# Expert weights in memory of their own, and the first expert unit chosen and turned while attention still runs

## The chip, the cores and the metric

The kernel runs on one core of a Trainium2 chip. The core has five engines that each take their instructions in order and wait for one another by semaphores: TensorE (PE, matrix products; PEld is its weight load), VectorE (DVE), ScalarE (ACT), GpSimd (POOL) and SyncE (SP, which here only starts DMAs). DMAs are started from SP, ACT and POOL. The metric is the time of one execution in device microseconds (us); lower is better. The kernel before took 1386.26 us, the median of three runs (1385.36, 1386.26, 1387.59).

## The reference: what is computed

Three stages follow one another, all in float32. The first is a decayed attention of 8 batches of 576 tokens with 8 heads of 64, the second a top-1 mixture of 8 experts (512 to 1024 to 512), the third a dense layer with a gate (512 to 2048 to 512).

```python
scores = scale * np.matmul(q, k.transpose(0, 1, 3, 2))
Dmat = np.where(rel >= 0, gamma[:, None, None] ** rel[None, :, :], 0.0)
x = np.matmul(scores * Dmat, v)                # then to (4608 tokens, 512)
logits = x @ w_gate + modality_bias[modality_id]
e_idx = np.argmax(logits, axis=1)              # gate_w: its softmax weight
for e in range(E):
    mask = e_idx == e
    out[mask] = gate_w[mask, None] * (np.maximum(x[mask] @ w1[e], 0.0) @ w2[e])
h = out @ w_in
result = (h - np.tanh(h)) @ w_out
```

Which tokens an expert gets is known only once attention and routing have run.

## The kernel before

**Attention.** 36 tiles of 128 tokens run in the loop of line 575, four tiles to a group (`RG`), groups 0 to 8. Tile `t` issues the scores of tile `t + 1` (`scores`), its own products (`attend`), the copy of its result to `xt` (`evac_x`, L433, on DVE), the scaling of a later tile's values on POOL, and the load of tile `t + 6` on SP (`load_tile`, six buffers from a pool). Routing of group `g - 1` is spread over the tiles of group `g`: `route_a` (logits, L464, copied by ACT at L467), `route_b` (turned, maximum, one-hot; L473 to L489), `route_c` (ranks by prefix sums, L498 to L516; L512 keeps the running counts `cum`). Then, a tile at a time, `scatter` writes token numbers into the slot table in DRAM by an indirect DMA on POOL (L520), and `store_x` turns a tile on PE (L531), scales it on ACT (L536, `save_x`) and writes it to `x_d`. The rule `due` doubles the scatters and stores up for group 6, so that tiles 24 to 27 are in DRAM early.

**The first unit.** An expert unit is up to 390 rows of one expert (`UE`); there are 12 of them, and a loop for what is left over. Since the first unit needs a full 390 rows before all are routed, `choose` (L436) takes the expert with the most rows among the first 28 tiles. Before, it stands at the end of tile 31. At tile 33 SP reads the choice into a register and loads the row numbers (`load_ids`, L199), and POOL fetches the rows in four pieces (`gather_rows`, L203; the last has 6 rows). After the last tile come the four turns of these rows on PE (`early`, L161, split by ACT at L162 and DVE at L163 into a high and a low float32r part), `route_a` of group 8, and the turn of tile 28.

**Expert units.** `blocks` (L700) runs steps `i` of (unit, f), f = 0 to 7. A step is 12 matmuls of 128x390 (L714: high by high, low by high, high by low, for four parts of the contraction), then `post` (relu on ACT at L824, low part on DVE at L825, weights of later steps split at L792 and L793), then `prep` (what else is due), and 12 matmuls of the second product of step `i - 2` (L943 to L945). The weights of a unit lie in `raw`, 16 pieces of 128x512, eight loads of 512 KB; `raw` and the split parts `wh` and `wl` came from pools opened after attention had closed its own. The first three loads of unit 0 were issued by SP after the last tile (L783), the other five by ACT in `post` of steps 0 and 1. The rest of the routing is hung into `prep` of unit 0: `rest_a` after step 0 (three scatters, `route_b` of group 8, two rows of stores), `rest_b` after step 1 (`route_c`, stores, four scatters), `rest_c` after step 2 (the counts by L642, `table`, L662 to L685 on DVE, which makes the list of units `utab`, and four stores), and then `swap`, which closes attention's right-hand pools. Unit 1's row numbers are loaded after step 2 (L199), its rows fetched after step 3 (L203) and turned after steps 6 and 7 (`tr_x`, L161). Later units fetch their rows in 13 pieces and turn them on DVE.

**PSUM.** Eight banks: in attention three for scores, two for the results, one for the state and two (`ps_m`) for routing and stores. In the units four are `hp` (a step's first product, and the tiles that `late_x` turns, in rotation) and four `acc`.

**The dense stage** (L982 to L1058) has 9 blocks of 512 tokens with 16 steps each; its weights `wout` (16 tiles) are loaded as it begins.

## Time and profile before

| | us |
|---|---|
| median of three runs | 1386.26 |
| lowest, highest | 1385.36, 1387.59 |
| the profiled execution | 1377.49 |
| its span, first to last instruction | 1375.8 |
| PE busy in the span | 1351.2 (98%) |
| DVE, ACT, POOL busy | 1041.5, 695.2, 330.5 |
| TensorE clock granted, mean | 0.997 of full |

The profile is of one execution, some 9 us below the median of the timed runs. Times in it count from the span's start. A row of the timeline gives the start, the time that it takes, the engine (with a q for what its queue issues), the line, the operation and its operands; `x8` is a merged row of eight; `[0.56 <-DVE rk L506]` is idle time of the engine just before it and what ended that. A float32 product of attention or a transpose by float32 counts several records. Ends on PE are modelled: two matmuls of 128x390 that follow each other start 0.18 us apart though each row says 0.34.

Attention takes the span up to 154.25 us, the units from 160.88 us to about 600 us, the dense stage the rest.

### The profile page before, as it was taken

The page shows a single profiled execution, that of the slowest core. Times are in us where ns is not written, and L with a number is a line of the kernel's source. Part 1 is how long each engine was busy: PE and PEld are TensorE (multiplying, and loading weights), DVE is VectorE, ACT ScalarE, POOL GpSimd, SP SyncE. Part 2 cuts the span into 40 slices and gives each one's busy share as a digit, 9 for nine tenths or more (in the row PEclk, how much of TensorE's full clock was granted, in tenths as well). Part 3 has the DMA queues.
Part 4 walks back from the last instruction along what each step waited for, and adds up shares of the span by engine and source line. Part 5 has one row for each costly group of instructions (what it writes and reads, how often), then busy time and mean ns, then how long its engine had stood idle before and what let it go on. Part 6 is the DMA issues. An engine that isn't in the chain of part 4 may idle for free.

```text
span 1375.8 us, 22319 instructions
## 1 busy us (share of the span) xinstructions
PE 1351.2 (98%) x8267; PEld 1186.1 (86%) x8267; DVE 1041.5 (76%) x1684; ACT 695.2 (51%) x1232; POOL 330.5 (24%) x381
## 2 busy tenths in 40 slices
PE   8999799999999999999999999999999999999998
PEld 7888699899999999988888888888888888888886
DVE  5766477798889888568778777786776877778775
ACT  3333344444444444456656556555555655555643
POOL 4555242443444444101101111011100111011101
PEclk9999999999999999999999999999999999999999
DMA  9998457444843446270100001000000000000000
GB/s 370 411 330 295 134 173 214 153 139 139 237 136 95 96 124 201 55 254 31 54 8 31 31 1 43 19 31 31 1 31 31 31 31 0 32 31 0 31 1 31
DMA packets 79726, 140.77 MB, mean 102 GB/s; under 512 B 36112, under 2 KB 42832, under 8 KB 79612
## 3 DMA queue, kind: packets, MB, share of 16 engines
q1 hardware_dynamic: 58780, 83.99, 18.7%
q10 hardware_dynamic: 12096, 35.45, 8.0%
q0 software_dynamic: 8736, 19.86, 4.3%
q8 instruction: 66, 1.08, 0.3%
q14 instruction: 48, 0.39, 0.1%
HBM read 133.29 MB, written 39.55 MB: 126 GB/s over the span
## 4 chain that ended last, share of the span: by engine, by line
PE 51%; issue 5%; POOL 0%; POOLq 0%; ACT 0%
PE hp L714 26%; PE acc L1021 8%; PE acc L1022 8%; PE acc L1023 8%; POOL out_dram L1047 0%; POOLq L1073 0%; ACT o L1044 0%; POOL nopt L1046 0%; POOLq L1037 0%; POOLq L1047 0%
## 5 line engine op out<-in xcount | busy, mean ns | idle before, releaser
L994 ACT ACTIVATE eh<-hp 128x512 f32<-128x512 f32 x144 | 86.1, 598 | 293.2 <-PE hp L714 274.9
L714 PE MATMUL hp<-xh,winh 128*128 128x512 f32 x576 | 224.1, 389 | 0.1
L1021 PE MATMUL acc<-wout,hi 128*128 128x512 f32 x576 | 224.2, 389 | 0.0
L1023 PE MATMUL acc<-wout,lo 128*128 128x512 f32 x576 | 224.2, 389 | 0.0
L1022 PE MATMUL acc<-wout,hi 128*128 128x512 f32 x576 | 224.1, 389 | 0.0
L714 PE MATMUL hp<-xl,winh 128*128 128x512 f32 x576 | 224.1, 389 | 0.0
L714 PE MATMUL hp<-xh,winl 128*128 128x512 f32 x576 | 224.1, 389 | 0.0
L996 DVE TENSOR_TENSOR el<-eh,hp 128x512 f32<-128x512 f32 x144 | 99.0, 688 | 156.5 <-ACT eh L995 156.5
L194 POOL DMA_INDIRECT xg<-x_d,idt x130 | 149.9, 1153 | 196.8 <-DVE lo L825 70.1
L742 POOL TENSOR_TENSOR xl<-yr,xh 128x512 fp32r<-128x512 f32 x36 | 49.2, 1366 | 429.2 <-ACT xh L741 429.2
L824 ACT ACTIVATE hi<-hp 128x390 fp32r<-128x390 f32 x96 | 47.7, 496 | 185.5 <-PE hp L714 132.5
L1005 DVE SCALAR_TENSOR_TENSOR el<-eh,el 128x512 f32<-128x512 f32 x144 | 128.6, 893 | 15.4 <-DVE el L1004 0.5
L714 PE MATMUL hp<-xh,wl 128*128 128x390 f32 x384 | 130.9, 341 | 3.4 <-DVE wl L793 3.4
L714 PE MATMUL hp<-xh,wh 128*128 128x390 f32 x384 | 132.0, 344 | 2.2 <-ACT wh L792 2.2
L714 PE MATMUL hp<-xl,wh 128*128 128x390 f32 x384 | 131.3, 342 | 0.2 <-issue 0.2
L943 PE MATMUL acc<-hi,wh 128*128 128x390 f32 x384 | 131.3, 342 | 0.0
L944 PE MATMUL acc<-lo,wh 128*128 128x390 f32 x384 | 130.5, 340 | 0.0
L945 PE MATMUL acc<-hi,wl 128*128 128x390 f32 x384 | 129.8, 338 | 0.2 <-issue 0.2
L714 PEld LDWEIGHTS hp<-xh,winh 128*128 128x128 f32 x576 | 108.2, 188 | 22.8 <-issue 0.4
L714 PEld LDWEIGHTS hp<-xh,winl 128*128 128x128 f32 x576 | 108.2, 188 | 22.6
L1022 PEld LDWEIGHTS acc<-wout,hi 128*128 128x128 f32 x576 | 108.3, 188 | 22.5
L1023 PEld LDWEIGHTS acc<-wout,lo 128*128 128x128 f32 x576 | 108.1, 188 | 22.7 <-DVE lo L1000 0.4
(169 smaller groups left out, 2611.9 us busy)
## 6 DMA issues: line engine op xcount, KB each, us to landing
raw<-in_w_dram SPq DMA_DIRECT2D x91, 512.0 KB
qk<-in_qk_dram SPq DMA_DIRECT2D x36, 512.0 KB
vk<-in_vk_dram SPq DMA_DIRECT2D x36, 512.0 KB
y_d<-yo SPq DMA_DIRECT2D x12, 780.0 KB
yr<-y_d SPq DMA_DIRECT2D x9, 1024.0 KB
raw<-in_wo_dram ACTq DMA_DIRECT2D x16, 512.0 KB
wo_d<-cv_em ACTq DMA_DIRECT2D x16, 512.0 KB
raw<-in_wi_dram ACTq DMA_DIRECT2D x16, 512.0 KB
```

The source lines that it names most:

```text
L194: nc.gpsimd.indirect_dma_start(out=dst, out_offset=None, in_=x_d[0:NT, :].rearrange("t (q c) -> (t q) c", q=NQ), in_offset=bass.IndirectOf ...
L714: nc.tensor.matmul(out=hp, lhsT=lhs, rhs=rhs, start=j == 0, stop=j == 3 * KD - 1)
L742: nc.gpsimd.tensor_tensor(out=yl[:, k], in0=yr[:, k], in1=yh[:, k].bitcast(F32), op=ALU.subtract)
L943: nc.tensor.matmul(out=o, lhsT=wh[:, cs], rhs=hi, start=first, stop=False)
L944: nc.tensor.matmul(out=o, lhsT=wh[:, cs], rhs=lo, start=False, stop=False)
L945: nc.tensor.matmul(out=o, lhsT=wl[:, cs], rhs=hi, start=False, stop=last)
L994: nc.scalar.activation(out=u, in_=hp, func=ACTF.Square)
L996: nc.vector.tensor_tensor(out=v, in0=u, in1=hp, op=ALU.mult)
L1005: nc.vector.scalar_tensor_tensor(out=v, in0=s, scalar=SQ_C, in1=v, op0=ALU.add, op1=ALU.mult)
L1021: nc.tensor.matmul(out=acc[s], lhsT=hi, rhs=wh, start=first, stop=False)
L1022: nc.tensor.matmul(out=acc[s], lhsT=hi, rhs=wl, start=False, stop=False)
L1023: nc.tensor.matmul(out=acc[s], lhsT=lo, rhs=wh, start=False, stop=last)
```

## The change

The weights of the first unit and the split buffers get memory that is taken at the start (`home`), so that their loads need not wait for attention's pools. The choice of the first unit moves from tile 31 to tile 30, the loading of row numbers and rows from tile 33 to tile 31, the eight weight loads into tiles 32 to 35 (all on ACT's queue), and three of the four turns into tiles 34 and 35. So that the choice can come earlier, routing of group 6 is pulled into tiles 28 and 29 (three scatters at tile 28, four at tile 29) and its stores into tiles 28 to 30. Routing of group 8 moves a step later: `route_a` after step 0, `route_b` after step 1, `route_c` inside `post` of step 2, the counts and `table` ahead of step 3; `swap` and unit 1's row numbers come after step 3. The first unit's rows now lie in a buffer of `xt` instead of two of the `vk` buffers. In the dense stage `raw` also serves as scratch, as input from block 1 on and as output buffer, six of the 16 `wout` tiles take the place of the split buffers, and the pool of `hi` and `lo` has three buffers instead of four.

```diff
+        home = pool("home", 1)
+        raw = home.tile([128, 2 * F1, DM], F32, name="raw")
+        w_b = [[home.tile([128, 2, DM], F32R, name=f"{n}{i}") for n in ("wh", "wl")] for i in range(3)]
...
+            def load_first(f):
+                nc.scalar.dma_start(out=raw[:, 2 * f:2 * f + 2].rearrange("p h c -> p (h c)"),
+                                    in_=A["w12"][bass.ds(first_act, 1), f, 0].rearrange("o p c -> (o p) c"))
...
+                soon = g == EARLY
                 if t + 1 < NTILE:
                     scores(t + 1)
+                if soon and r == 0:
+                    ls_box[g - 1] = route_a(g - 1)
+                if t == NTILE - 2:
+                    turn_rows(0, 0, x0[0], ps_sc.tile([128, KD, TL], F32, name="sc"))
+                if t == NTILE - 1:
+                    for s in range(1, SE - 1):
+                        turn_rows(0, s, x0[s], ps_m.tile([128, KD, TL], F32, name="m"))
                 attend(t)
...
+                if soon and r == 0:
+                    route_b(g - 1, ls_box.pop(g - 1))
+                    for w in range(t - RG - 3, t - RG):
+                        scatter(w)
+                elif soon and r == 1:
+                    route_c(g - 1)
+                    for w in range((g - 1) * RG, g * RG):
+                        scatter(w)
...
+                    for w in ([w], [w, w + 1], [w + 1, w + 2, w + 3], [])[r] if soon else [w]:
+                        store_x(w)
-                if t == (EARLY + 1) * RG - 1:
+                if t == EARLY * RG + 2:
                     choose()
-                if t == (EARLY + 1) * RG + 1:
+                if t == EARLY * RG + 3:
                     base = nc.sync.value_load(pick[0:1, 0:1], min_val=0, max_val=(E - 1) * CAP)
-                    first = nc.sync.value_load(pick[0:1, 1:2], min_val=0, max_val=E - 1)
                     first_act = nc.scalar.value_load(pick[0:1, 1:2], min_val=0, max_val=E - 1)
...
+                if t >= EARLY * RG + 4:
+                    for f in ((0,), (1, 2), (3, 4), (5, 6, 7))[t - EARLY * RG - 4]:
+                        load_first(f)
+                if t >= NTILE - 2:
+                    split_w((t - NTILE + 2, 0))
...
-            early(0)
-            early(1)
-            ls_last = route_a(g)
-            for s in range(2, SE):
-                early(s)
-            t_ahead = late.pop(0)
-            tp_ahead = turn_x(t_ahead, False)
             c1.close()
...
+                    else:
+                        for _ in range(2):
+                            h_p.tile([128, UB], F32, name="hp")
+                        t = late.pop(0)
+                        tp = turn_x(t, True)
+                        turn_rows(0, SE - 1, x0[SE - 1], h_p.tile([128, UB], F32, name="hp").rearrange("p (k t) -> p k t", k=KD))
+                        ahead.extend((t, tp))
+                        split_w((2, 0))
+                    blocks(names, F1, 2, UE, xT, lambda i: rest_c() if idt is None and i == 3 else None, g1w, gemm2e, post, prep, finish)
```

PE at the end of attention, before: the last scores (L364), the products of tiles 34 and 35 (L400, L408), then the turns of the first unit's rows (L161, three full pieces and one of 6 rows), the logits of group 8 (L464), the turn of tile 28 (L531) and the first matmul of step 0 (L714).

```order
L364 MATMUL sc<-qk 128x128 x8
...
L400 MATMUL xp<-qk,state_112 64x128 x8
L408 MATMUL xp<-a,vs 64x128 x8
L161 MATMUL sc<-ident,vk 128x128 x8
L464 MATMUL m<-xt,wg 32x512 x4
L161 MATMUL sc<-ident,vk 128x128 x4
L161 MATMUL xp<-ident,vk 128x6 x4
L531 MATMUL m<-ident,xt 128x128 x4
L714 MATMUL hp<-xh,wh 128x390
```

The same place of the changed kernel, where the turn is L166, scores are L384, products L420 and L428, the turn of a stored tile L551 and the step L746.

```order
L384 MATMUL sc<-qk_143 128x128 x8
L166 MATMUL sc<-ident,xt 128x128 x4
...
L166 MATMUL m<-ident,xt 128x128 x8
L420 MATMUL xp<-qk_143,state_122 64x128 x8
L428 MATMUL xp<-a,vs_153 64x128 x8
L551 MATMUL hp<-ident,xt 128x128 x4
L166 MATMUL hp<-ident,xt 128x6 x4
L746 MATMUL hp<-xh,wh_73 128x390
```

Twelve of the sixteen turns now stand ahead of the last products, and the logits of group 8 have left this place.

ACT from the last turn to step 2, in the changed kernel: the split of the turned rows is L167, that of weights L177, the relu L842, the copied logits L487, the stored rows L556, the exponential of routing L503.

```order
L167 CAST xh<-hp 128x4x6
L177 CAST wh_77<-raw 128x512
L842 ACTIVATE hi<-hp 128x390
L177 CAST wh_73<-raw 128x512
L487 COPY ls<-m 128x512
L556 ACTIVATE xo<-hp,gate 128x4x4x32 x2
L842 ACTIVATE hi<-hp 128x390
L177 CAST wh_75<-raw 128x1024
L503 ACTIVATE ex<-lg 128x32
L556 ACTIVATE xo<-hp,gate 128x4x4x32 x2
L842 ACTIVATE hi<-hp 128x390
```

The first stored tile, turned ahead of step 0 in a bank of `hp`, is now read by ACT only behind step 0's relu, a split and the copy of the logits.

## Rows read from the trace of the kernel before

**Rows 1.** The page, part 2: PE's busy tenths in 40 slices of the span.

```profile
PE   8999799999999999999999999999999999999998
```

**Rows 2.** Windows: stretch, its length, busy us and (records) by engine, clock, DMA.

```profile
141.15:154.25 13.10, 10.84 (x181) 7.97 (x179) 6.93 (x22) 1.93 (x5) 4.91 (x6) 1.00 0.24 64
154.25:160.88 6.63, 3.62 (x31) 2.11 (x29) 2.69 (x5) 2.90 (x7) 3.38 (x8) 1.00 0.68 216
160.88:174.65 13.77, 12.42 (x75) 11.48 (x75) 8.75 (x25) 7.88 (x13) 1.62 (x3) 0.88 0.64 222
174.65:191.80 17.15, 17.15 (x99) 17.12 (x98) 11.44 (x34) 6.15 (x9) 7.16 (x9) 1.00 0.71 219
264.90:272.00 7.10, 3.90 (x13) 3.75 (x13) 7.03 (x13) 3.17 (x6) 0.33 (x1) 0.76 0.53 149
```

**Rows 3.** Timeline of PE, end of attention to the first matmul of step 0.

```profile
140.64 0.59 PE L423 MATMUL st<-vs,vk 128*64 128x64 f32 x13 [1.11 <-issue]
...
150.45 0.76 PE L408 MATMUL xp<-a,vs 128*64 128x128 f32 x9 [0.45 <-issue]
...
152.57 0.67 PE L400 MATMUL xp<-qk,state 64*64 64x128 f32 x16 [0.56 <-DVE rk L506]
153.16 1.09 PE L408 MATMUL xp<-a,vs 128*64 128x128 f32 x16
154.19 1.09 PE L161 MATMUL sc<-ident,vk 128*128 128x128 f32 x8
...
156.08 1.06 PE L464 MATMUL m<-xt,wg 128*32 128x512 f32 x8 [0.80 <-DVE xt L433]
...
157.66 0.41 PE L161 MATMUL xp<-ident,vk 6*128 6x6 f32 x4
...
160.88 0.45 PE L714 MATMUL hp<-xh,wh 128*128 128x390 f32 x1 [2.21 <-ACT wh L792]
```

**Rows 4.** Timeline of DVE and ACT: evacuation of a tile, logits, splits, a store, relu.

```profile
120.15 0.69 DVE L433 TENSOR_TENSOR xt<-xp,gx 128x512 f32<-128x512 f32 x1 [0.36 <-PE xp L408]
...
159.15 0.58 ACT L467 COPY ls<-m 128x512 f32<-128x512 f32 x1 [0.96 <-PE xp L161]
...
160.11 0.20 ACT L162 CAST xh<-xp 128x24 fp32r<-128x24 f32 x1
160.18 1.16 ACT L792 CAST wh<-raw 128x512 fp32r<-128x512 f32 x2
...
168.18 0.67 ACT L536 ACTIVATE xo<-m,gate 128x512 f32<-128x512 f32 x1
...
169.32 0.49 ACT L824 ACTIVATE hi<-hp 128x390 fp32r<-128x390 f32 x1
```

**Rows 5.** Timeline: routing of group 8, the table, unit 1's row numbers and turn.

```profile
167.05 0.28 DVE L477 TENSOR_REDUCE lg<-m 128x32 f32<-128x128 f32 x1
...
168.49 0.19 DVE L489 TENSOR_TENSOR oh_all<-riota,cm 128x32 bf16<-128x32 f32 x1
...
172.92 0.17 PE L642 MATMUL m<-cum,ones 128*128 128x8 bf16 x1 [0.83 <-DVE cum L512]
...
174.88 0.15 DVE L662 COPY vals<-m 1x8 f32<-1x8 f32 x1
...
180.00 0.13 DVE L685 CAST nreg<-incl 1x1 int32<-1x1 f32 x1
...
180.77 0.40 SPq L199 DMA_DIRECT2D idr<-slot_d  x1
...
191.80 1.04 PE L161 MATMUL hp<-ident,xg 128*128 128x128 f32 x8
```

**Rows 6.** Timeline: the choice, the first unit's row numbers, and its last gather.

```profile
136.35 0.13 DVE L450 CAST pick<-star 1x1 int32<-1x1 f32 x1
...
140.93 0.41 SPq L199 DMA_DIRECT2D idt<-slot_d  x1
...
148.50 0.90 POOL L203 DMA_INDIRECT vk<-x_d,idt  x1 [0.31 <-issue]
```

More of the change, by code (lines that the diff above doesn't have):

```diff
@@ L756 @@
                 cvs2, fill2 = [], []
-                raw = raw_p.tile([128, 2 * F1, DM], F32, name="raw")
-                wsp, xg, regs, yos = {}, {}, {}, {}
-                steps = [(u, f) for u in range(UMIN) for f in range(F1)]
+                xg, regs, yos = {}, {}, {}
                 limits = {0: E * CAP, 1: E - 1, 2: NT, 3: 1}
@@ L949, in run_units @@
                         gather(names[0], idt)
-                    for f in range(F1 if idt is not None else 3):
-                        load_raw(f)
-                    split_w((0, 0))
                     if idt is not None:
+                        for f in range(F1):
+                            load_raw(f)
+                        split_w((0, 0))
                         for s in range(SE):
```

133 lines of the change are left out of this document (66 added, 67 removed).

## The prediction

> **What bounds the kernel now.** I read the page's slices first: PE is busy in nearly all of them and dips in only three places, at the start, in slices 3 and 4 (about 103 to 172 us) and near 265 us [rows 1]. So PE's order of work sets the end, and a change to any other engine counts only through a pause of PE. Next come the windows over the join of attention and units [rows 2]. From 154.25, where the last products of attention end, to 160.88, where the first expert matmul starts, PE is busy 3.62 of 6.63 us. From there to 174.65, the start of the first second product, the granted clock is 0.88, a mean of the two levels 2.4 and 1.2 GHz. From 174.65 on PE has no gap at full clock: 99 records in 17.15 us, 0.173 each (I use 0.18 for a matmul, so 2.15 for twelve). What the change can win lies between about 120 and 175 us.
>
> The timeline says what ended last at the join [rows 3, 4]. After the products (153.16 + 1.09) PE does sixteen turns and the logits. Then ACT, in its own order, copies logits (159.15), splits the last turned piece (160.11) and only then the weights (160.18); PE idles 2.21 us for that. The weights are ready when ACT comes to them, since no DMA is named: it is ACT's queue, not the load, that is late.
>
> **The change, part by part.** The sum is made in the profiled execution, 1377.49 us (1375.8 of span and 1.7 around it); I subtract the same amount from the median of 1386.26, which stands 8.8 higher.
>
> *The join.* What is left behind the last products is: DVE takes the last tile out of PSUM, 0.36 after them and 0.69 long [rows 4]; that frees the bank in which the 6-row piece is turned, 0.41 [rows 3]; ACT splits it in 0.20 [rows 4], and with about 0.2 for each of the two hand-overs to ACT and back, and 0.2 more for the last turn's drain, the first matmul comes 2.1 us after the products instead of 6.63. The turn of tile 28 runs beside the evacuation. Weights of steps 0 and 1 are split in tiles 34 and 35, ahead of that. The twelve other turns are not gone: eight take 1.09 [rows 3], so twelve take about 1.4, now on PE in tiles 34 and 35. There two of them stand between the products of tile 34 and 35, where PE waited 0.56 for DVE [rows 3]; that wait goes. So 6.63 - 2.1 - 1.4 + 0.56 = 3.7 us gained. Bounds: 1.5, if ACT's three DMA issues of tile 35 (an issue of SP or POOL holds its queue 0.4 to 0.9 [rows 5, 6]) push the split of the last piece back by 2; 4.7, if the last turn needs no wait at all (1.05 less).
>
> *The earlier choice.* Tile 30 now stores three tiles and makes the choice, through two banks. The third turn waits until ACT has scaled the first (0.67 [rows 4]) and the counts for the second; one turn is 0.45, so I put 0.5 of new waiting on PE, between 0 and 1.4 (two whole scalings). Scatters and stores are as many as before. Routing of group 6, moved up, waits for nothing that is later than a score product. What is late next is the gather: before, the choice was written at 136.35, row numbers were asked for at 140.93 and the last gather left POOL at 149.4 [rows 6], while the first turn stood at 154.19 [rows 3]. In the new order the choice comes one tile (4 us) earlier and the scatters before it are already out, so the gather should end by about 143, the first turn comes near 147: 4 us of margin. Cost 0, bound 2.
>
> *The weight loads.* Eight loads of 512 KB move from 155 to 172 us into tiles 32 to 35. There DMA was busy 0.24 of the time [rows 2], 4 MB of new traffic fits in the 13 us beside 64 GB/s of old (together 384 GB/s if all of it came there), and the last five are wanted only from step 3 on. SP loses three issues and a register load, ACT gets all eight. 0, bounds 0 and 1.
>
> *Steps 0 to 7 of the first unit.* The routing of group 8 starts one step later, though the units cannot be listed without it. By the rows, from the first matmul as zero: step 0 ends at 2.15; ACT does relu (0.5), a split (0.58), the copy of the logits (0.58) and the stored tile 28 (0.67) by 4.5 [rows 4]; only then is the bank free that step 1 writes, since tile 28 was turned into it. PE would be ready at 3.65 (logits 1.06 [rows 3], four turns 0.45), so it waits 1.1: a new wait. Step 1 ends at 6.9, relu, a split of two pieces (1.1, by the two of 1.16 in [rows 4]) and its low part (about 1.2, two passes of DVE like the 0.69 of [rows 4] less a start) hold DVE until 9.9, then the 1.6 us of `route_b` (from L477 at 167.05 to the end of L489 at 168.68 [rows 5]) bring the one-hot at 11.45. PE, with turns and step 2, is ready at 10.35: it waits 1.1 more, against 0.36 before. The counts are now behind twelve matmuls of the second product, so their wait of 0.83 [rows 5] goes. Table from 15.2, 5.2 us long (174.88 to 180.1 [rows 5]), ends at 20.4. PE reaches the turn of unit 1 at 30.6. Before it was 191.80 - 160.88 = 30.9, with a low clock in it that cost 0.12 x 13.77 = 1.65 [rows 2]. So 0.3 gained, if the clock stays high. Without the waits PE would gain 2.2 more; if they come and the clock falls all the same, 1.65 less.
>
> *Unit 1's rows.* From the table's end to the turn it was 191.80 - 180.1 = 11.7 us [rows 5], now 30.6 - 20.4 = 10.2. The turn showed no wait, and its first two pieces are the first two of four gathers, so some of the 11.7 was slack; I take 0, the bound is 1.5.
>
> *The dense stage.* Scratch in `raw`, other places of `wout` and three `hi`/`lo` buffers: a buffer is rewritten after the first product of a step, and the second product that read it stands on PE ahead of that one. Six `wout` tiles load behind the last unit and are wanted from step 10 of the first block. 0 both ways; if its cover goes, one load of 512 KB, some 2 us.
>
> Sum: 3.7 - 0.5 + 0.3 = 3.5 us less: 1374.0 in the profiled execution, 1382.8 on the median. 3.5 us is 0.25%, and 0.2% (2.8 us) is about what a measurement of this kernel can tell from no change, so the forecast lies just over that line.
>
> **Rivals.**
>
> 1. *The gain stays but half of it goes back in steps 0 to 2.* The two new waits of 1.1 us, with the idle time around the 6-row turn, leave PE with pauses in the place where the clock was low before. For it: after the 2.21 us of idle time the stretch ran at 0.88. Against it: between 141.15 and 154.25 PE was busy only 10.84 of 13.10 and had 1.00 [rows 2]. With 1.65 lost: 1384.4. The Trainium skill, "TensorE: Matmul & The Clock Gate", HAM oscillation, says that PE's pauses for data bring the lower clock back each time, which would speak for this rival; the trace agrees only for the pause of 2.21 us and that at 265 us (0.76), and shows full clock over the shorter ones. By the rule the sum is 1.9, by the trace 3.5.
> 2. *Slower: unit 1's rows come too late.* The chain from the logits of group 8 over the table to the gather is all latency, and the change starts it a step later. If the rows land more than 10.2 us after the table, PE stops at the turn, in order, with all behind it; and the next unit's gather starts only when these rows are turned. What a late gather costs is seen at 265 us: 13 records in 7.10 us instead of 2.3, so 4.8 [rows 2]. Two of these less 3.5 make +6.1: 1392.4. For it: fewer us are left than before. Against it: DMA carries no expert weights there now, and no wait showed at 191.80.
> 3. *The choice is not early enough.* If the first rows land after tile 34's scores, PE waits inside attention and the gain is moved, not won. It decides from 4 us of lateness on; at 7 us it takes back the whole 3.5: 1386.3. Against it: nothing else is on SP or POOL after tile 31.
> 4. *More than forecast.* In tiles 32 and 34 PE stands still between records of one product, with nothing named: 1.11 before 140.64 and 0.45 before 150.45 are the last of several such gaps [rows 3], together some 2.5 and 1.9 us by the idle part of those tiles (2.26 of 13.10 in the window [rows 2]). They lie beside the bursts of scatters and gathers, which the change moves away. If they go: 1382.8 - 4 = 1378.8. Against it: the bursts go to tiles 28, 29 and 31, where the gaps may follow.
>
> **How the numbers follow.** Forecast 0.42, rival 1 0.26, rival 2 0.12, rival 3 0.08, rival 4 0.12. The forecast's own range, from its bounds, is 1380.5 to 1385.5, and about two thirds of it is over 2.8 us: 0.29; with rival 4 and a sixth of rival 1, faster has 0.46. Rival 2 and half of rival 3 give slower 0.16, with a little for the terms that I cost at nothing 0.18. The rest, 0.36, is within 0.2%. The range goes from 1378.0, below rival 4, to 1389.0, between rivals 3 and 2; outside lie most of rival 2 and a tail below.
>
> **What the profile after would show.** The first expert matmul about 2 us after the last product and without an ACT wait on weights; turns between the products of tiles 34 and 35, none waiting for a DMA; a wait of about 1 us on ACT before step 1 and on DVE before the prefix matmuls; PEclk 1.00 there; no wait at unit 1's turn; the window from the last product to that turn some 4 us shorter. A low clock after the join would speak for rival 1, a turn that waits for a DMA for 2 or 3, tiles 32 and 34 of under 4 us for 4. The forecast is wrong if the join takes over 5 us still, or if steps 0 to 7 take over 33.

## The result: 1.05% slower, by a new wait of the dense stage and by rows of indirect DMAs

The changed kernel takes 1401.54 us (median of 6 runs, 1396.99 to 1406.38) against 1386.92 of the kernel before in the same set: ratio 1.0105, interval 1.0081 to 1.013, 14.6 us slower. The prediction was 1382.8 with a range up to 1389.0; it is wrong, in sign too. The profiled execution of the changed kernel took 1398.16 us (span 1396.0).

One sentence is needed for all that follows: in some sets of runs the kernel before takes 1387 to 1389 us, in others 1375 to 1377, and a time is therefore compared only with the runs of before in its own set.

Three stages, cut at two instants that both traces have (start of the first expert matmul; end of the last unit's copies, ACT's `yo`), with two repeats of each kernel:

| profile | first step starts | from there to last copies | from there to last product | own time |
|---|---|---|---|---|
| before | 160.88 | 425.5 | 783.7 | 1377.49 |
| after | 164.25 | 434.3 | 792.3 | 1398.16 |
| before, second | 160.72 | 430.4 | 783.8 | 1382.30 |
| after, second | 165.10 | 433.3 | 791.8 | 1397.11 |
| before, third | 153.43 | 433.4 | 783.7 | 1377.97 |
| after, third | 152.63 | 427.9 | 791.8 | 1379.27 |

The last stage is 8.0 to 8.6 us longer in every pair. The first is 3.4 and 4.4 longer in two pairs and 0.8 shorter in the third. The middle varies by more in one kernel than between the two.

**Profile after.** Part 2 of its page, TensorE and its granted clock (answers to [rows 1]). Counted from 0, slice 4 (139.6 to 174.5 us) still dips, and new dips stand in slice 15, with the stop at 552.76 below, and in slice 17, where the dense stage begins.

```profile
PE   8999899999999998989999999999999999999998
...
PEclk9999899999999999999999999999999999999999
```

Windows of the changed kernel: from the last product to the first step, the first two steps, from the last unit's copies to the first product with `wout`, and the 6.5 us behind (columns as in [rows 2]).

```profile
159.24:164.25 5.01, 1.19 (x11) 0.85 (x9) 2.58 (x6) 1.17 (x4) 3.18 (x6) 0.85 0.94 297
164.25:178.04 13.79, 12.91 (x74) 10.89 (x74) 5.76 (x17) 6.30 (x12) 0.00 (x0) 0.81 0.23 91
596.45:614.53 18.08, 12.71 (x57) 10.17 (x55) 3.83 (x6) 5.99 (x12) 0.00 (x0) 0.97 0.40 135
614.53:621.00 6.47, 6.27 (x16) 4.50 (x17) 5.60 (x10) 4.13 (x7) 0.00 (x0) 0.57 1.02 418
```

The join takes 5.0 us instead of the 2.1 of the prediction, and the steps behind it run at 0.81 of full clock, lower than the 0.88 of [rows 2]. What ended last there, in the order PE, DVE, POOL (start, duration, what it waited for):

```profile
158.15 1.09 PE L428 MATMUL xp<-a,vs 128*64 128x128 f32 x16
159.18 0.66 PE L551 MATMUL hp<-ident,xt 128*128 128x128 f32 x4
163.39 0.59 PE L166 MATMUL hp<-ident,xt 6*128 6x6 f32 x4 [3.56 <-DVE xt L453]
164.25 0.69 PE L746 MATMUL hp<-xh,wh 128*128 128x390 f32 x1 [0.27 <-ACT xh L167]
```

```profile
159.23 1.28 DVE L168 TENSOR_TENSOR xl<-m,xh 128x512 fp32r<-128x512 f32 x2
162.64 0.69 DVE L453 TENSOR_TENSOR xt<-xp,gx 128x512 f32<-128x512 f32 x1 [2.13 <-remote]
```

```profile
157.65 1.03 POOL L540 DMA_INDIRECT slot_d<-tokid,pos_s  x1 [8.95 <-DVE co L531]
...
161.73 0.96 POOL L540 DMA_INDIRECT slot_d<-tokid,pos_s  x1 [0.19 <-issue]
```

The last products should have ended at 159.24, and the next ones, the turn of tile 28 (L551), start at 159.18 right behind them. Yet DVE could take the result only at 162.64, "remote": its one wait, on PE's semaphore, ended then, and the trace records that event at 162.62. So at this place the products are not late, only their signal. A row of four scatters runs on POOL from 157.65 to 162.69. The evacuations of the last tiles (DVE's `xt`, start in us) show delays at other rows too; the last column belongs to the run with two scatters per tile, below:

| tile | before | before, third | after | after, third | scatters two per tile |
|---|---|---|---|---|---|
| 28 | 120.15 | 120.49 | 121.07 | 120.87 | 122.79 |
| 29 | 124.91 | 125.25 | 127.23 | 125.07 | 126.73 |
| 30 | 129.11 | 129.45 | 134.81 | 129.42 | 131.81 |
| 31 | 133.25 | 133.60 | 141.91 | 135.97 | 137.66 |
| 32 | 140.88 | 138.53 | 146.64 | 138.53 | 140.48 |
| 34 | 151.74 | 146.33 | 156.09 | 147.09 | 150.91 |

In tiles 28 to 31 of the changed kernel stand a row of three (122.81 to 126.35) and of four scatters (129.05 to 133.86); by tile 31 it is 8.7 us behind. In the kernel before the row of four runs from 134.99, behind the evacuation of tile 31, and tile 32 is late there. Tile 31 of the third profile after (135.97) is the change's own order and no row: DVE makes the choice ahead of that evacuation. Tile 32 is level again, at 138.53 in both kernels.

The dense stage. ACT of the changed kernel, then of the kernel before, from the last copies to the first evacuation; then SP of the changed kernel and of the kernel before.

```profile
596.45 2.08 ACT L940 COPY yo<-acc 128x390 f32<-128x390 f32 x4 [3.27 <-PE acc L964]
608.72 0.60 ACT L1021 ACTIVATE raw<-hp 128x512 f32<-128x512 f32 x1 [10.19 <-SPq L994]
```

```profile
584.25 2.09 ACT L921 COPY yo<-acc 128x390 f32<-128x390 f32 x4 [3.27 <-PE acc L945]
588.98 0.60 ACT L994 ACTIVATE eh<-hp 128x512 f32<-128x512 f32 x1 [2.64 <-PE hp L714]
```

```profile
598.56 0.41 SPq L860 DMA_DIRECT2D y_d<-yo  x1
599.30 0.96 SPq L861 DMA_DIRECT2D tok_d<-slot_d  x1
608.87 4.57 SPq L780 DMA_DIRECT2D wout<-wo_d  x9
```

```profile
586.37 0.42 SPq L843 DMA_DIRECT2D y_d<-yo  x1
587.12 0.96 SPq L844 DMA_DIRECT2D tok_d<-slot_d  x1
595.94 4.67 SPq L748 DMA_DIRECT2D wout<-wo_d  x9
```

Before, ACT takes the first dense result 2.6 us behind its copies. Now it waits 10.2 us, until SP passes L994, the end of the loop that may follow the units. Two transfers are on their way there: the last `y_d` store, issued at 598.56, and behind it the copy of 390 single ids to `tok_d`, issued at 599.30. By the landing events of the trace the store had landed at 604.73 and the ids at 608.23; SP's next load goes out at 608.87. So it is the copy of the ids that lands last, 3.5 us behind the store. In all twenty profiles of this case the ids land behind the store, and SP goes on 0.5 to 0.8 us behind the ids; in the kernel before SP waits just as long, but nothing on ACT waits with it. TensorE fills its four banks and stops:

```profile
614.53 0.80 PE L1048 MATMUL acc<-wout,hi 128*128 128x512 f32 x1 [5.22 <-ACT hi L1026]
```

The 5.2 us of stop and some 2.8 us for the clock behind it (0.57 over 6.47 us) make 8.0 of the 8.6 us.

The middle. In this profile TensorE stopped once for 5.03 us, at 552.76, for a gather that came late (DVE waits for it):

```profile
549.09 0.71 DVE L186 STREAM_TRANSPOSE xg<-xg 128x512 f32<-128x512 f32 x1 [8.63 <-DMA xg<-x_d,idt]
```

### The profile page after: what moved, and what is told of

Its sections match the earlier page's. It is cut to its first block, busy times and chain, and to the rows that moved or that the text cites. A ratio compares the mean times of both kernels' runs of the same rounds, so it can differ in the third digit from the quotient of the medians.

```text
span 1396.0 us, 22336 instructions
## 1 busy us (share of the span) xinstructions
PE 1360.9 (97%) x8267; PEld 1191.2 (85%) x8267; DVE 1042.3 (75%) x1685; ACT 695.8 (50%) x1233; POOL 331.7 (24%) x381
## 4 chain that ended last, share of the span: by engine, by line
PE 50%; issue 5%; POOL 0%; DVE 0%; POOLq 0%; ACT 0%; DVEq 0%
PE hp L746 25%; PE acc L1050 8%; PE acc L1049 8%; PE acc L1048 8%; POOL out_dram L1074 0%; POOLq L1100 0%; DVE raw L1033 0%; DVE raw L1032 0%; DVE raw L1024 0%; DVE lo L1027 0%; ACT raw L1022 0%; DVE raw L1023 0%; ACT raw L1071 0%; POOL nopt L1073 0%; POOLq L1064 0%
## 5 line engine op out<-in xcount | busy, mean ns | idle before, releaser
L1021 ACT ACTIVATE raw<-hp 128x512 f32<-128x512 f32 x144 | 86.4, 600 | 304.8 <-PE hp L746 281.3
L746 PE MATMUL hp<-xh,winh 128*128 128x512 f32 x576 | 224.1, 389 | 0.1
L746 PE MATMUL hp<-xh,winl 128*128 128x512 f32 x576 | 224.1, 389 | 0.0
L746 PE MATMUL hp<-xl,winh 128*128 128x512 f32 x576 | 224.1, 389 | 0.0
L1023 DVE TENSOR_TENSOR raw<-raw,hp 128x512 f32<-128x512 f32 x144 | 99.1, 688 | 164.8 <-ACT raw L1022 164.8
L1048 PE MATMUL acc<-wout,hi 128*128 128x512 f32 x360 | 141.2, 392 | 5.2 <-ACT hi L1026 5.2
L842 ACT ACTIVATE hi<-hp 128x390 fp32r<-128x390 f32 x96 | 47.7, 497 | 190.4 <-PE hp L746 148.7
L1050 PE MATMUL acc<-wout,lo 128*128 128x512 f32 x360 | 141.0, 392 | 0.2 <-DVE lo L1027 0.2
L1049 PE MATMUL acc<-wout,hi 128*128 128x512 f32 x360 | 141.0, 392 | 0.0
L1032 DVE SCALAR_TENSOR_TENSOR raw<-raw 128x512 f32<-128x512 f32 x144 | 128.5, 893 | 15.4 <-DVE raw L1031 0.5
L746 PE MATMUL hp<-xh,wl 128*128 128x390 f32 x384 | 132.6, 345 | 7.2 <-DVE wl L178 7.2
L774 POOL TENSOR_TENSOR xl<-raw,xh 128x512 fp32r<-128x512 f32 x32 | 43.0, 1344 | 395.4 <-ACT xh L773 395.4
L746 PE MATMUL hp<-xh,wh 128*128 128x390 f32 x384 | 132.5, 345 | 0.8 <-issue 0.4
L746 PE MATMUL hp<-xl,wh 128*128 128x390 f32 x384 | 131.1, 341 | 0.2 <-DVE xl L168 0.2
L178 DVE TENSOR_TENSOR wl<-raw,wh 128x1024 fp32r<-128x1024 f32 (+1 forms) x99 | 117.6, 1188 | 14.7 <-ACT wh L177 12.8
L746 PEld LDWEIGHTS hp<-xh,winh 128*128 128x128 f32 x576 | 108.2, 188 | 23.0 <-issue 0.4
L746 PEld LDWEIGHTS hp<-xl,winh 128*128 128x128 f32 x576 | 108.2, 188 | 22.4
L746 PEld LDWEIGHTS hp<-xh,winl 128*128 128x128 f32 x576 | 108.0, 188 | 22.4
```

Of the source, the lines that this page charges most:

```text
L178: nc.vector.tensor_tensor(out=wl[:, 0:n], in0=r, in1=wh[:, 0:n].bitcast(F32), op=ALU.subtract)
L746: nc.tensor.matmul(out=hp, lhsT=lhs, rhs=rhs, start=j == 0, stop=j == 3 * KD - 1)
L1021: nc.scalar.activation(out=u, in_=hp, func=ACTF.Square)
L1023: nc.vector.tensor_tensor(out=v, in0=u, in1=hp, op=ALU.mult)
L1032: nc.vector.scalar_tensor_tensor(out=v, in0=s, scalar=SQ_C, in1=v, op0=ALU.add, op1=ALU.mult)
L1048: nc.tensor.matmul(out=acc[s], lhsT=hi, rhs=wh, start=first, stop=False)
```

## The experiments

Theories: **T1**, a row of indirect DMAs on POOL holds TensorE's small products back, or their signals (a hold, below); **D**, the dense scratch in `raw` waits for the last store (by the landings above, for the ids behind it); **G**, the units' late gathers are a matter of their own. Rivals are named at each run.

**What comes again.** The changed kernel once more:

> The changed kernel once more, with a second profile. Its first profile lost 20.2 us against the kernel before: a join of 5.0 us from the last product to the first step, with half clock behind it (162.7 to 169.5), a stop of 5.22 us at the first dense products (614.5) with half clock, a stop of 5.03 us in the seventh unit (552.8, a late gather) with half clock, and half clock in tiles 30 and 31 (135.4 to 142.2). Theory: the join, the dense stop and the slow stretch of tiles 30 and 31 are made by the order of the program and come again at the same places within 1 us; the stop in the seventh unit is a straggling gather and comes at another unit or not at all, which makes the spread of the runs (1397 to 1406 us). Rival: all four come again at the same places, and the late gather belongs to the change too.

Measured 1401.17 us, 1.0086 (1.0043 to 1.0129). Join and dense stop came again (4.37 and 4.92 us of stop), the late gather moved to 382 (5.10 us). Half clock in tiles 30 and 31 came again shorter (138.1 to 141.5). The theory holds. The kernel before once more:

> The kernel before once more, for a second profile. By its first one: first step at 160.88, 425.5 us from there to the end of the last unit's copies, 783.7 us from there to the last product. Theory: first step and dense stage come again within 1 us; the middle part varies by 8.5 us for each late gather (a stop of 5 to 6 us and 6.8 us at half clock), at whatever unit it falls. Rival: the kernel before has no such stops of 5 us, only the changed kernel has them.

Measured: first step 160.72, dense stage 783.8, and a stop of 5.43 us at 546 behind a late gather. The rival falls: the kernel before has such stops too.

**The dense stage.** Scratch of the first four steps in memory of its own, three `wout` tiles loaded later into it:

```diff
+                own = [e_p.tile([128, 3, UB], F32, name=n) for n in ("eh", "el")]
+                    eh, el = own if i < 4 else (raw[:, 0:3], raw[:, 3:6])
```

> The changed kernel, but the dense stage's scratch (eh, el) lies for its first four steps in memory of its own, and only then in the raw tile; the last three wout tiles load at step 5 into that memory. Theory D: in the changed kernel ScalarE's first dense evacuation waited until 608.72, 12.3 us behind the last unit's copies, because it writes into raw, which DMAs of the loop behind the units could have written, and so waits for the last y_d store's queue to land; TensorE filled its four banks and stopped for 5.22 us, and half clock for 6.8 us followed (3.4 us lost). Without that, first evacuation 4.5 to 5 us behind the copies as before, no stop, no half clock: 8.6 us less than the changed kernel, near 1393. Rival R: the stop comes from the three instead of four hi/lo buffers, which are kept here: the stop of 5 us stays and the time is that of the changed kernel, 1401.

Measured 1399.72 us, 1.0086 (1.0041 to 1.0132); the stop was 3.76 us and the dense stage 790.2. Its trace says why so little came of it. ACT:

```profile
594.27 0.60 ACT L1024 ACTIVATE eh<-hp 128x512 f32<-128x512 f32 x1 [2.67 <-PE hp L746]
...
601.43 0.72 ACT L1033 ACTIVATE el<-eh,epsb 128x512 f32<-128x512 f32 x1 [5.47 <-SPq L994]
```

`eh` is free at once, `el` waits for the same event: it lay over `yo`, which that store reads. So the place of the scratch decides, and this place was no better. Moved on by 2432 bytes (the text below says 15 KB, the edit 608 numbers of 4 bytes):

> As the run with the dense stage's scratch in its own memory, but moved by 15 KB: there el lay over the tile yo, which the last y_d store still reads, and so VectorE and ScalarE waited until the store had landed (601.43) all the same. Theory D: with neither raw nor yo under them, the first evacuation comes 2.6 us and the first product with wout 10.6 us behind the last unit's copies, as in the kernel before; no stop of TensorE, no half clock, the dense stage takes 783.7 us instead of 792.3: 8.5 us less than the changed kernel. Rival R (three hi/lo buffers): a stop of 4 us or more stays, the dense stage takes 790.

Measured 1392.54 us, 1.003 (0.9994 to 1.0067). ACT and PE:

```profile
595.37 0.60 ACT L1025 ACTIVATE eh<-hp 128x512 f32<-128x512 f32 x1 [2.67 <-PE hp L746]
```

```profile
603.40 0.50 PE L1057 MATMUL acc<-wout,hi 128*128 128x512 f32 x1
```

First evacuation 2.67 behind the copies, first `wout` product 10.7 behind them (10.6 in the kernel before), no stop, no half clock, though the ids landed as late as ever; rival R falls, since the three buffers are still there. The stage took 786.6, not 783.7: 0.3 us in each of nine blocks, with `wout` products at 391 ns instead of 389. With 2560 bytes instead (below) it was 784.2.

**The rows.** Group 7's four scatters leave the join, each behind a small copy on POOL that waits for step 1 or 2:

```diff
+                            nc.gpsimd.tensor_copy(out=nopt, in_=(hi, lo)[w][:, 0:1].bitcast(F32))
+                            scatter(NTILE - RG - 6 + 2 * steps[i][1] + w)
```

> The changed kernel, but the four scatters of group 7 (tiles 28 to 31) leave the join: each waits on GpSimd for a value of unit 0's step 1 or 2 (two and two). Theory T1: a row of four indirect DMAs on GpSimd (157.65 to 162.7) held back TensorE's last products, so that VectorE's last evacuation came at 162.64 and not at 160.5. Without the row the first step starts 2 to 3 us earlier (near 161.5), and TensorE's clock does not fall to half for 6.8 us: 5.5 to 6 us less than the changed kernel, near 1395.5. Theory T2: the eight weight loads (DMA engines 97% busy from 156 to 164) held it back; the evacuation stays at 162.6, the first step at 164, the time at 1401.

Measured 1401.88 us, 1.0093 (1.0054 to 1.0132). The time does not show it (four stops of 2.7 to 6.1 us in the units of its profile), the place does. PE and DVE:

```profile
158.95 1.09 PE L428 MATMUL xp<-a,vs 128*64 128x128 f32 x16
...
161.97 0.41 PE L166 MATMUL hp<-ident,xt 6*128 6x6 f32 x4 [1.34 <-DVE xt L453]
```

```profile
161.24 0.68 DVE L453 TENSOR_TENSOR xt<-xp,gx 128x512 f32<-128x512 f32 x1
```

DVE waits no more; first step at 162.65, 2.6 us behind the products, though the loads keep the DMA engines as busy. The run with all three cures, further down, has the same edit and 2.4 us. The rival's own run, half of the loads issued later:

> The changed kernel, but four of the first unit's eight weight loads are issued behind step 0 and not in tile 35, the other four one or two tiles earlier at the latest; the scatters stay at the join. Theory T2 (the loads hold the last products back): DMA engines nearly idle from 157 to 163, last evacuation at 160.6, first step near 161.5, 5.5 us less, near 1396. Theory T1 (the row of scatters does it): the evacuation comes at 162.6 and the first step at 164 as in the changed kernel; the time is 1401, or 1 to 2 us more where steps 4 to 7 wait for their weights.

Measured 1399.53 us, 1.0079 (1.0035 to 1.0123): evacuation at 161.68, first step at 163.37, 4.4 us behind the end of the products, against 5.0 and 5.8 in the two profiles of the changed kernel and 2.6 without the row. T1 carries most; that the loads have a part, of about 1 us by these single profiles, is likely and not shown. Then the other rows, two scatters per tile:

> The changed kernel, but the seven scatters that it issues in rows of three and four in tiles 28 and 29 are spread over tiles 27 to 31, two per tile. The row at the join stays. In the changed kernel VectorE's evacuations of tiles 28 to 32 come at 121.1, 127.2, 134.8, 141.9 and 146.6, against 120.2, 124.9, 129.1, 133.3 and 140.9 in the kernel before, and TensorE has half clock from 135.4 to 142.2. Theory T1 (rows of indirect DMAs hold TensorE back): evacuation of tile 32 at 141 to 143, no half clock there, first step near 160, 4 us less than the changed kernel. Rival T3 (the routing and the stores of three tiles, moved up, are the work that slows these tiles): evacuation of tile 32 stays at 146, half clock stays, time unchanged.

Measured 1390.18 us, 1.0026 (0.9978 to 1.0073); evacuations in the table above, tile 32 at 140.48, no half clock there, first step at 159.83. T3 falls. And the price by itself, in the kernel before:

> The kernel before with work added in the steady part of attention, where a tile takes 3.9 us and one indirect DMA per tile is issued anyway: in tile 10 a row of four more indirect DMAs on GpSimd (128 rows of 64 bytes each, into memory that nothing reads), in tile 14 four DMAs of as many rows of as many bytes on SP's queue, in tile 18 five multiplications on GpSimd (5.2 us of it) without any DMA, in tile 22 a row of eight indirect DMAs. Read by how late VectorE's evacuations come against the kernel before. Theory T1 (a row of indirect DMAs itself holds TensorE's many small products back): 2 to 4 us behind the row of four, 5 to 9 behind the row of eight, under 0.5 behind the other two. Rival T4 (GpSimd is busy and late with its own products): as much behind tile 18 as behind tile 10. Rival T5 (512 small packets crowd the DMA engines): as much behind tile 14 as behind tile 10.

Measured (1404.79 us in one run). DVE's evacuations of tiles 16 and 28 in this run, then in the second profile of before:

```profile
79.33 0.69 DVE L437 TENSOR_TENSOR xt<-xp,gx 128x512 f32<-128x512 f32 x1 [0.35 <-PE xp L412]
...
137.64 0.69 DVE L437 TENSOR_TENSOR xt<-xp,gx 128x512 f32<-128x512 f32 x1 [0.35 <-PE xp L412]
```

```profile
73.27 0.69 DVE L433 TENSOR_TENSOR xt<-xp,gx 128x512 f32<-128x512 f32 x1 [0.36 <-PE xp L408]
...
120.77 0.69 DVE L433 TENSOR_TENSOR xt<-xp,gx 128x512 f32<-128x512 f32 x1 [0.36 <-PE xp L408]
```

As lateness of evacuations against the second profile of before: 6.1 us behind the row of four (tile 16), no more behind SP's four (tile 18: 6.1), behind the arithmetic 1.3 for one tile and none after it (tile 20: 6.2), behind the row of eight 10.6 more (tiles 25 to 28: 16.9). T4 and T5 fall. The lateness has half clock in it, from 64.1 to 70.9 behind the row of four and from 111.9 to 122.1 at the row of eight. Ahead of the row of eight TensorE starts 165 products in 8.5 us, beside it 27 in 10:

```profile
98.00:106.50 8.50, 8.50 (x165) 7.27 (x163) 7.32 (x22) 1.57 (x5) 6.00 (x10) 1.00 0.96 339
108.00:118.00 10.00, 5.79 (x27) 3.82 (x26) 0.69 (x1) 0.00 (x0) 7.38 (x13) 0.69 0.47 153
```

```profile
108.24 0.35 PE L427 MATMUL st<-vs,vk 128*64 128x64 f32 x4 [0.38 <-issue]
109.00 0.33 PE L427 MATMUL st<-vs,vk 128*64 128x64 f32 x3 [0.40 <-issue]
```

Three or four products, a pause without a named cause, again: that is how a held TensorE looks in these rows, and [rows 3] had it at 140.64 and 150.45.

**All three cures**, then the gathers apart too, then in pairs:

> The changed kernel with all three edits: scatters of tiles 21 to 27 spread, the four scatters of group 7 moved behind steps 1 and 2, the dense stage's scratch in memory that no late DMA touches. If the three losses are what the theories say (about 4, 3 plus 1.7 for the clock, and 8.5 us): first step near 158.5, dense stage 783.7 us, and 15 to 17 us less than the changed kernel: near 1385, 0.1 to 0.4% below the kernel before in the same conditions. Rival: the loss lies in the unit stage, whose late gathers the change makes more frequent; then the time stays above that of the kernel before by 5 us or more, with two or more stops of 5 us in the units.

> As the run with all three edits, and besides the four gathers of the first unit, a row from 143.8 to 148.6 before, wait each for the evacuation of one more tile; and the dense scratch is moved on by 128 bytes (there the nine wout products of the last three steps of a block lay at an address of 19 times 128 bytes and took 391 instead of 389 ns on average, 0.3 us a block). Theory T1: the stops at 145 to 147 (1.4 us in the first of these runs) go, first step 1.5 to 2 us earlier, near 154.6; dense stage 783.7 instead of 786.0; 4 us less than that run, near 1382. Rival: the stops beside the gathers come from the first weights' loads at the same time; first step stays at 156.4.

> As the run with the gathers apart, but in two pairs: the first two at once, the last two behind the evacuation of tile 33 (144.6 there). In that run the last gather waited for tile 34's evacuation and landed after 154, and the 6-row turn waited 2.07 us for it (first step 156.71). Theory: the pairs hold TensorE for less than 0.5 us each, the last gather lands before 151, the 6-row turn waits for the last evacuation alone, first step 154.5 to 155.3: 1.5 to 2 us less than that run, 0.5 to 0.7% below the kernel before. Rival: a pair costs as much as half a row (1.5 us); then the first step stays past 156.

Measured: the first 1386.31 us, 0.9987 (0.995 to 1.0024), first step 156.39, 2 us earlier than forecast and 7.9 earlier than in the changed kernel. The second 1381.46 us, 0.994 (0.9899 to 0.9982), first step 156.71 and not 154.6: the stops beside the gathers went, but the last gather came 2.07 us late for its turn. The third 1377.22 us, 0.9998 (0.9974 to 1.0022), first step 152.66; in its set the kernel before took 1377.36, and as the last three runs below show, such a set has 152.6 without any mending, so the pairs are not tested by it. In all three the units took 433 to 438 us.

**The kernel before without rows:**

> The kernel before with only its scatters moved: group 6's four, a row from 135 to 139.8 there, wait for evacuations of tiles 31 and 32, and group 7's four at the join wait for steps 1 and 2. Nothing of the change is in it. If the rows are what costs, tile 32's evacuation comes at 137 to 138 instead of 140.9 and the first step at 156 to 157.5 instead of 160.9: 3 to 5 us less than the kernel before, and what the change's own idea (choice, weights and turns earlier) still gains against it in the run with all three edits is 0 to 1.5 us. Rival: the earlier turns are what gains; then the first step here stays past 159.

> The kernel before with all its rows broken up (group 6's scatters, group 7's at the join, and the four gathers in two pairs, the second behind tile 34's evacuation), and nothing of the change. In the run with its scatters moved, the row of gathers stood in the way instead and stopped TensorE for 4.34 us at 152.6. Theory: that stop goes, first step 156 to 157.5, 3.5 to 4.5 us less than the kernel before; against it the change's own idea (earlier choice, weights and turns ahead of the last products) gains 1 to 2.5 us in the run with paired gathers. Rival: without the earlier turns and weights the join keeps its 6.6 us and the stop only moves; first step past 159, and the idea gains 4 us or more.

Measured 1385.19 us, 0.996 (0.9927 to 0.9994): tile 32 at 140.18 and first step at 160.50, a miss, since the row of gathers now held the last tile (a stop of 4.34 us at 152.6). And 1384.60 us, 1.0048 (1.0024 to 1.0073), in the set of 1377: first step 155.81, as forecast, yet the turns waited 2.58 us for the second pair of gathers (at 154.6), and the delayed scatters made unit 1's gather late, two stops of 1.87 and 2.23 us at 189 and 192. Where nothing is held, breaking the rows up in this way cost 7.2 us.

**The units.** Rows of SP and POOL in the changed kernel before its stop at 552.76:

```profile
537.15 0.36 SPq L860 DMA_DIRECT2D y_d<-yo  x1
537.89 0.97 SPq L861 DMA_DIRECT2D tok_d<-slot_d  x1
```

```profile
539.57 1.11 POOL L211 DMA_INDIRECT xg<-x_d,idt  x1 [0.30 <-issue]
```

The POOL row is the last of 13 gathers. A unit's store and its 390 single ids go out between the last gathers of the next rows. One edit, in either kernel:

```diff
-                    if f == 3 and u - 1 in yos:
+                    if f == 5 and u - 1 in yos:
```

> As the run of the changed kernel with paired gathers (first step 152.66, which is 8.2 us earlier than in the kernel before, and yet the same time as the kernel before), but a unit's y_d store and its copy of 390 ids are issued in step 5 of the next unit, not in step 3, where the last of the 13 row gathers are still under way (store at 537.2 and ids at 537.9 against last gather at 539.6 in the changed kernel). Theory G (the gain is given back in the unit stage, where store and ids hold the last gathers' packets up: a stop of 5 to 7 us and 6.8 us at half clock each): the stops of 3 us and more in units 2 to 11 go, units 420 to 422 us from first step to last copies, time 1364 to 1368. Rival: stops come all the same, at other units (late for another reason); time 1374 to 1378.

> The kernel before with the same one edit (store and ids in step 5). Theory G: its stops in the units (3.2 at 268, 5.4 at 546 in its two profiles) go too, 1371 to 1373 by its profile's stages (first step 160.9, dense stage 783.7, 7.4 us outside, units 419.5), so that the changed kernel with its three losses mended keeps 5 to 8 us of lead against it. Rival: no change in time, and no lead that can be measured.

Measured 1365.30 us (1365.08 to 1365.72), 0.993 (0.9907 to 0.9953), and 1364.05 us (1363.61 to 1364.78), 0.992 (0.9897 to 0.9944). No stop of 0.5 us or more in units 2 to 11 of either profile; units 420.5 and 419.3 us. G holds, and with the late gathers the spread of the times is gone. But the kernel before gains as much, and its first step stood at 153.77 with its rows unmoved. What decides that, the program or the set?

> The kernel before, a third profile. In the last set of runs its times were 12 us lower than in the sets before (median 1375 against 1387 to 1389), and in that set the kernel before with its stores issued later had no product held back beside its rows of indirect DMAs (tile 32's evacuation at 138.6, first step at 153.8), though the rows were there. Theory C (the state of the chip decides whether a row holds TensorE back): where the kernel before runs near 1375, its evacuation of tile 32 comes at 138.6 and its first step at 153.8, with its rows unmoved; where it runs near 1387, at 140.9 and 160.8. Rival P (something in the program with the later stores removes the hold): 140.9 and 160.8 whatever its time.

> The changed kernel, a third time. The dense stage's wait is the program's own: 792 us there against 783.7 in the kernel before, in any state of the chip, so that it is slower by at least 8 us less what the join gains. Theory C: in a state without holds the evacuations of tiles 28 to 32 come like the kernel before's (tile 32 within 1.5 us of it), the first step 1 to 4 us before the kernel before's, and the whole is 5 to 8 us slower (0.4 to 0.6%). In a state with holds: first step 164 to 165, 12 to 15 us slower (1%).

> The changed kernel with a unit's store and ids issued in step 5 instead of step 3, and nothing else. Without the late gathers' stops its time is nearly fixed, and against the kernel before with the same edit (1364.05; first step 153.8, units 419.3, dense stage 783.8) it shows what the change itself costs: dense stage 792 (8.4 us more), first step 152 to 154 in a state without holds (0 to 2 us gained) or 164 to 165 with them, units 419 to 421. So 1370 to 1373 without holds, near 1384 with them. Rival: the change also makes gathers late in the units; then the units take 424 us or more.

Measured: the kernel before, unedited, at 138.53 (tile 32) and 153.43 (first step):

```profile
138.53 0.67 DVE L433 TENSOR_TENSOR xt<-xp,gx 128x512 f32<-128x512 f32 x1
```

```profile
153.43 0.45 PE L714 MATMUL hp<-xh,wh 128*128 128x390 f32 x1 [0.75 <-ACT wh L792]
```

So the set decides, not the program; C holds, P falls. It is not the chip either: the chips numbered 6 and 15 each have sets of both kinds, while the four sets with holds are the earlier ones and the three without are the later ones. The changed kernel 1383.23 us, 1.0059 (1.0034 to 1.0083); its join with the same row of four scatters beside it:

```profile
149.15 1.09 PE L428 MATMUL xp<-a,vs 128*64 128x128 f32 x16
150.18 0.66 PE L551 MATMUL hp<-ident,xt 128*128 128x128 f32 x4
151.96 0.41 PE L166 MATMUL hp<-ident,xt 6*128 6x6 f32 x4 [1.12 <-DVE xt L453]
152.63 0.45 PE L746 MATMUL hp<-xh,wh 128*128 128x390 f32 x1 [0.27 <-ACT xh L167]
```

With the later store the changed kernel takes 1371.47 us (1370.12 to 1372.67), 0.9965 (0.995 to 0.9981): first step 153.41, units 420.2, dense stage 791.4. Against 1364.05 of the kernel before with that edit (another set, in the same state by its first step) that is 7.4 us, and the dense stage alone differs by 7.6.

The fastest version that ran is thus the kernel before with the later store. The mended changed kernel with it lies 1.3 us higher in the same set: first step 0.7 earlier, dense stage 0.5 longer, and 1.2 longer in the units, where the turns of unit 1 wait twice (0.65 and 0.69 us) for rows that the mending delays. What the change's idea is worth where nothing is held is that 0.7, or the 0.8 of the third pair of profiles, or the 0.4 of the two kernels with the later store alone (153.77 and 153.41). Two profiles of the changed kernel's unedited attention differ by 0.8 (152.63 and 153.41), so a gain under 1 us is all that can be said.

## Why the prediction was wrong, step by step

*The dense stage* is the step that failed. It was put at 0, "0 both ways", on an argument about buffers that are rewritten and one load. It looked at who reads the scratch later, not at who wrote the memory before: `raw` is a target of DMAs in the loop behind the units, and the next writer waits until SP has passed that loop, with the last store and the ids on its queue. What the runs showed instead is a wait of ACT for SP, 10.2 us, until the copy of the ids behind the last store has landed, and with it a stop of TensorE of 5.2 us: 8.0 to 8.6 us in every pair, in any set. Its bound ("some 2 us") was the price of a load; the nearest row would have been SP's own wait in the kernel before, from the ids at 587.12 to the next load at 595.94.

*The join* was mis-sized. Its terms (0.36, 0.69, 0.41, 0.20, two hand-overs and a drain of 0.2 each) add up to 2.26 and not to the 2.1 written. Without holds the stretch from last product to first step was 2.39, near it by luck in part: DVE took the last tile 0.98 behind the products (151.22) and not 0.36, since it still split the rows turned in tile 35, a term that the sum lacks, while the hand-overs cost less. The turns moved forward cost 1.3 where the sum had 1.4. But the 6.63 us from which the sum starts held 2.1 us of hold, as the kernel before has 4.5 there without it. So the gain is 0.8, not 3.7. With holds the row of four scatters, which in the kernel before runs beside turns, falls on the last products' signal: 5.0 us, and first step 3.4 later than before instead of 3.2 earlier.

*The earlier choice.* 0.5 predicted, between 0 and 1.4; without holds tile 32's evacuation comes at 138.53 in both kernels, so 0, within the bounds. With holds it came 5.8 us late. The sentence that scatters are "as many as before" was true and missed the point, since three and four of them now stood in a row. Rival 4 named these pauses and even that "the bursts go to tiles 28, 29 and 31", and gave them 0.12 and only a gain.

*Steps 0 to 7.* Turn of unit 1 predicted 30.6 behind the first step; 29.6 without holds at full clock, 31.9 in the first profile, where the clock was 0.81. Of the two new waits of 1.1, that on ACT ahead of step 1 came in no profile of the changed kernel, and that on DVE ahead of the prefix matmuls was 0.87. The Trainium skill, "TensorE: Matmul & The Clock Gate", HAM oscillation, which rival 1 leant on, says that pauses bring the lower clock back; the traces agree for every stop of 2.9 us and more at the join, and for three of five between 1.1 and 1.4 us: the stop of 1.12 in the third profile above had full clock behind it.

*Unit 1's rows, weight loads*: the turn of unit 1 waited in no profile of the changed kernel, and no weight was late; both right.

*The reading of the page.* The slices of [rows 1] dip below 9 inside the span only in slice 4 (137.6 to 172.0 us). The dip at 265 us that the prediction names is in the window of [rows 2] and not in the slices; the slip carries nothing.

For the 14.6 us of the medians that leaves 8.6 shown at the dense stage and 3.4 at the first step; the other 2.6 lie in the units, where late gathers make more difference from run to run than that. That the change adds to them there is not shown and not excluded; with the later store, and without holds, the units of the two kernels take 420.2 and 419.3 us.

**Open.** Why a row of indirect DMAs holds TensorE in some sets and not in others. The Trainium skill, "SBUF — State Buffer", Who interferes with whom, says that a DMA never contends with a computing engine for that memory; the later sets agree (tile 32 level at 138.53), and in the earlier ones, with 27 products in 10 us where 165 in 8.5 went before, no run shows whether memory is what they wait for. Small products are not a condition: the units have such pauses too, with their long matmuls, up to this one in the run with later loads, beside gathers issued at 473.92 and 475.17.

```profile
474.98 0.45 PE L965 MATMUL acc<-hi,wh 128*128 128x390 f32 x1 [2.04 <-issue]
```

Two signs separate the two kinds of sets. From 60 us to the end of the units, all 13 profiles of the earlier sets have pauses of TensorE that end by "issue", without a named cause, and none of the 7 later ones has any. And of the landing events of the indirect DMAs, sixteen for each, the first profile of the kernel before has 1576 of 3360 on record and its third has 3353; all 13 of the earlier sets have 1397 to 1746, the 7 later ones 3316 to 3353. Whether the signals themselves were crowded, as the late one at the join suggests, or the recording of them held the engine up, no run tells: every execution on record carries a span and a granted clock, so none is known to have run without recording, and the recording stays an untested rival.

## What to carry to other kernels

Memory that is given a second use brings the waits of its first: ask which queue wrote or read it last, not only who needs it next. Work that is moved is priced with what stands beside it at the new place. A row of small asynchronous requests is broken up only where a run shows that it holds something: spread, the scatters of tiles 28 and 29 gave 4.4 us at the first step where they held, and breaking up the rows of the kernel before cost 7.2 us where they did not. Where times scatter, look for the one late transfer that makes them scatter before a 3 us change is judged by them: here two steps of delay for a store and its copy of ids took 11 us and the scatter away.

## What the runs showed of the hardware

A row of four indirect DMAs on POOL (1.26 us apart) cost attention 6.1 us and a row of eight 10.6, half clock included, in a set that held; in another set on the same chip rows of four cost nothing that the evacuations show. A copy of 390 single ids, issued 0.7 us behind a store of 780 KB, landed 1.7 to 4.3 us behind it, 8.0 to 9.5 us after its own issue. With 2432 bytes ahead of the scratch and of the three late `wout` tiles, most products of three steps of a block took 392 to 398 ns, which makes 391 the mean of all; with 2560 bytes, and in the kernel before, every one took 389.
